# Packed weights shared by batches 0 and 1 from block 1 on, a one-instruction gate in units 10–28, 115–128 and 180–255, and moved plan times

## The chip, the cores and the metric

The kernel runs on one core of one Trainium2 chip. The metric is device time in microseconds (us), the median of three runs. Five engines work side by side, each through its own queue in order: PE (TensorE, matrix products), DVE (VectorE), ACT (ScalarE), POOL (GpSimd) and SP (SyncE, which here only issues DMAs). All share the core's 16 DMA engines.

## The reference, cut to what matters

Two attentions in a row, then two feed-forward layers, all in f32:

```python
p_packed = sm_attn(p, k, v)            # 32 packed queries a head, over 576 keys
out = sm_attn(q, p_packed, p_packed)   # 576 queries over those 32
x = out as (8*576, 8*64)               # 4608 tokens, 512 features
h = x @ w_in                           # 512 -> 2048
g = h * (1 / (1 + exp(-1.702 * h)))    # the gate
x = g @ w_out                          # 2048 -> 512
h = max(x @ w1, x @ w2, x @ w3)        # 512 -> 768
out = h @ w_out2                       # 768 -> 512
```

Batch 8, heads 8, head width 64.

## The kernel before

**Numbers.** Every f32 operand of a large product is split into a high and a low part, and `mm3` (lines 97 to 102) makes three matmuls of it: high by low, low by high, high by high.

**Packed weights.** The second attention's output is never multiplied with `w_in` itself. `p_packed` of a batch is multiplied with `w_in` once, which gives the packed weights `pw[b, n]` of batch b and block n (512 of the 2048 hidden features; n is 0 to 3). The first feed-forward product of the batch is then attention weights (`at`) by `pw`. Two code paths make `pw`. For batches 2 to 7, `pw_unit` (line 402) takes two batches at once: their packed rows stand interleaved in a tile `sp`, so three matmuls of 512 columns serve a pair, and the result is evacuated in two halves of 64 partitions, each by an ACT copy (high part) and a DVE subtraction (low part). For batches 0 and 1, `pw1_unit` (line 418) works on one batch: its tiles `pt` hold zeros beside the packed rows, so six matmuls are made where the pair path makes three, and the evacuation is over 128 partitions at once. Both paths take their accumulator from `ps_a`, two PSUM tiles that the attention's scores, transposes and sums also use.

**Units.** The first feed-forward layer runs in 256 units n of (batch, half of the tokens, 128 hidden features). `h_unit` makes six matmuls of 288 columns (`h<-at,pw`) into one of two PSUM tiles, ACT takes a tanh of it and DVE joins both to `(1 + tanh) * h` (lines 460, 461), which is twice the gate. `g_unit` splits that: ACT writes the high part, DVE (POOL for the first two units) the low part. `out_unit` makes twelve matmuls (`acc<-g,wo`), two units later on PE, and halves the sum when it evacuates it. Batches 0 and 1 hold units 0 to 63, in the pattern batch 0 block 0, batch 1 block 0, batch 0 block 1, batch 1 block 1, then blocks 2 and 3 of batch 0 (from unit 32) and of batch 1 (from unit 48).

**The start.** Weights are converted on the chip from the 32-bit form they arrive in (`convert`, `convert_low`: chains of DVE instructions over 128x1024 with two ACT passes). In the first 60 us DVE converts the first blocks of `w_in` and `w_out` while it also runs the softmaxes of the attention groups (batch, half of the heads): (0,0), (0,1), (1,0), (1,1). The exponentials are ACT's `Exp` (lines 259 and 340).

**What sets the order.** Every piece of work is put into `plan` with a time, and the plan is recorded in order of time (`main`, lines 804 to 925): tables such as `D_`, `K_`, `L_`, `W_`, `Q_` and `R_` shift single steps. A scheduler then settles each engine's own order. Nothing waits for a clock: an instruction runs when those ahead of it on its engine are issued and its inputs are there. The second feed-forward layer (`Set`, `out2`) takes the last 550 us; no line of it is touched.

Of the kernel before, what the change touches and what calls it, by code (L numbers as in the profile page):

```python
# [19 lines left out]
P = 128  # L20
# [10 lines left out]
SCALE = 1.0 / D ** 0.5  # L31
D_ = [-2, -8, 2.9, -2.51, 2.83, -0.47, -3.58, -0.6, 0.92, -0.32, -6.66, 0.91, 2.97, 2.32, -5.59, -0.32]
W_ = [60, 15.02, 42.09, 0]
K_ = [2, 11, -8, 6, 1, -7, 10, 6, -11, -14, -9, -5, -2, -13, -1, 4]
L_ = [8.18, 16.49, 4, 22.39]
Z_ = [1, 1, 1, 0, 0, 0, 0, 0, 0, 0, 0, 0, 0, 0, 0, 0]
PL_ = [10, 12]
Q_ = [12, 9, 9, 8]
R_ = [32, 23, 17, 5]
TP_ = [6.0, 8.5, 5.0]  # L40


@with_exitstack
def tile_packed_attention_moe(
# [159 lines left out]
    class Group:  # L204
# [91 lines left out]
        def pt(self):  # L296
# [86 lines left out]
    def pw_unit(pr, c, n):  # L383
# [65 lines left out]
    part = {}  # L449

    def h_unit(n):
        b, hf, fc = units[n]
        o = ps_h.tile([P, TB], F32, tag="ph", name=f"h_{n}")[:, :HALF]
        hs = slice(hf * HALF, hf * HALF + HALF)
        fs = slice(fc % 4 * P, fc % 4 * P + P)
        for g in range(2):
            w = pw[b, fc // 4][:, g]
            mm3(o, (w[:, 0, fs], w[:, 1, fs]), [t[:, hs] for t in at[b, g]], g == 0, g == 1)
        t = gp.tile([P, HALF], F32, tag="t", name=f"t_{n}")
        nc.scalar.activation(t, o, AF.Tanh, scale=0.5 * 1.702)  # L460
        nc.vector.scalar_tensor_tensor(out=t, in0=t, scalar=1.0, in1=o, op0=ALU.add, op1=ALU.mult)  # L461
        gt[n] = t

    def g_unit(n):
        g = gp.tile([P, 2, HALF], F32R, tag="g", name=f"g_{n}")
        latest["act"] = nc.scalar.copy(g[:, 0], gt[n])  # L466
        eng = nc.gpsimd if n < 2 else nc.vector
        latest["dve"] = eng.tensor_tensor(out=g[:, 1], in0=gt[n], in1=f(g[:, 0]), op=ALU.subtract)  # L468
        gt[n] = g

    def out_unit(n):
# [3 lines left out]
        for dc in range(KD):  # L475
# [328 lines left out]
    def main():  # L804
        HU = 2.2
        T0 = 39

        add(-2.0, keep_busy, 28)
        attention(0.0, 0, 0, 1.07)
        attention(8, 0, 1, 1.07)  # L810
        attention(20, 1, 0, 0.97, 0)
        attention(34, 1, 1, 0.97, 0)

# [3 lines left out]
        for n in range(N1 + 2):  # L817
# [30 lines left out]
        for n in range(NQ):  # L848
# [3 lines left out]
            for g in range(2):  # L852
# [68 lines left out]
        for n in range(9 * NBLK):  # L921
# [85 lines left out]
```

## Time and profile before

| | |
|---|---|
| median of 3 runs | 1334.27 us (1333.46 to 1334.63) |
| the profiled execution, its own time | 1333.64 us |
| its span (first to last instruction) | 1331.5 us |
| PE busy | 1308.8 us, 98% |
| DVE busy | 919.9 us, 69% |
| ACT busy | 533.3 us, 40% |
| POOL busy | 107.4 us, 8% |
| instructions | 22347 |

Busy is the time in which an engine has an instruction at work, and a busy PE is not PE at its peak, since matmuls overlap. How long a matmul holds PE is read from the distance between two starts. Idle time of an engine counts only where another waits for it.

### The profile page before, as it was taken

How to read it: one execution, taken by the hardware profiler on the slowest of the kernel's cores; microseconds unless marked ns; L12 is line 12 of the kernel's file. 1: busy time of each engine (PE TensorE's matmuls, PEld its weight loads, DVE VectorE, ACT ScalarE, POOL GpSimd, SP SyncE). 2: the span in 40 equal slices, each digit the busy share in tenths (PEclk: the TensorE clock that was granted, in tenths of full speed). 3: DMA queues.
4: the chain of work that ended last, by engine and by line, in shares of the span. 5: the costliest groups of instructions: out<-in, count | busy, mean ns of one | idle time of the engine just before them, and what ended most of it. 6: DMA issues, size and time to landing. Idle time of an engine off the chain costs nothing.

```text
span 1331.5 us, 22347 instructions
## 1 busy us (share of the span) xinstructions
PE 1308.8 (98%) x8614; PEld 1229.7 (92%) x8614; DVE 919.9 (69%) x1896; ACT 533.3 (40%) x1140; POOL 107.4 (8%) x218
## 2 busy tenths in 40 slices
PE   6899999999999999999999999999999999999998
PEld 5699898989999989999999999999899899999997
DVE  6899976874756565669999889736556467366461
ACT  3466544554445444446656442311311313123111
POOL 1200001100000000000000001001011011010000
PEclk9899999999999999999999999999999999999999
DMA  9697734643323331236655649847657476575451
GB/s 338 211 403 300 251 107 139 193 123 120 106 80 100 103 102 54 82 112 195 207 200 191 206 160 360 294 169 252 223 188 264 151 261 239 172 254 197 174 174 48
DMA packets 88875, 249.70 MB, mean 188 GB/s; under 512 B 10177, under 2 KB 39361, under 8 KB 81857
## 3 DMA queue, kind: packets, MB, share of 16 engines
q0 software_dynamic: 24640, 132.66, 29.2%
q1 hardware_dynamic: 64128, 115.62, 25.4%
q8 instruction: 68, 1.11, 0.3%
q14 instruction: 39, 0.31, 0.1%
HBM read 204.47 MB, written 43.78 MB: 186 GB/s over the span
## 4 chain that ended last, share of the span: by engine, by line
PE 92%; DVE 4%; DMA 2%; issue 1%; ACT 1%; SPq 0%; POOL 0%; ACTq 0%; DVEq 0%; POOLq 0%
PE acc L100 10%; PE p L101 10%; PE p L100 10%; PE p L102 10%; PE acc L102 10%; PE acc L101 9%; PE h L100 5%; PE h L102 5%; PE h L101 5%; PE accb L101 4%; PE accb L102 4%; PE accb L100 4%; PE pw L100 1%; PE pw L101 1%; PE pw L102 1%; PE pv L287 1%
## 5 line engine op out<-in xcount | busy, mean ns | idle before, releaser
L100 PE MATMUL acc<-g,wo 128*128 128x288 f32 x1024 | 303.6, 299 | 0.0
L102 PE MATMUL acc<-g,wo 128*128 128x288 f32 x1024 | 300.6, 294 | 0.0
L101 PE MATMUL acc<-g,wo 128*128 128x288 f32 x1024 | 299.6, 293 | 0.4 <-POOL g L468 0.3
L100 PEld LDWEIGHTS acc<-g,wo 128*128 128x128 f32 x1024 | 191.4, 188 | 10.5 <-issue 5.3
L101 PEld LDWEIGHTS acc<-g,wo 128*128 128x128 f32 x1024 | 192.2, 188 | 4.3 <-issue 1.0
L102 PEld LDWEIGHTS acc<-g,wo 128*128 128x128 f32 x1024 | 192.0, 188 | 1.6 <-issue 1.5
L460 ACT ACTIVATE t<-h 128x288 f32<-128x288 f32 x256 | 104.8, 410 | 181.7 <-PE h L102 179.8
L461 DVE SCALAR_TENSOR_TENSOR t<-t,h 128x288 f32<-128x288 f32 x256 | 114.7, 450 | 84.7 <-ACT t L460 83.3
L100 PE MATMUL h<-at,pw 128*128 128x288 f32 x512 | 155.2, 304 | 1.3 <-DVE t L461 1.1
L101 PE MATMUL h<-at,pw 128*128 128x288 f32 x512 | 151.7, 296 | 0.3 <-POOL at L125 0.3
L102 PE MATMUL h<-at,pw 128*128 128x288 f32 x512 | 151.3, 296 | 0.0
L466 ACT CAST g<-t 128x288 fp32r<-128x288 f32 x256 | 110.6, 433 | 93.6 <-DVE t L461 92.4
L468 DVE TENSOR_TENSOR g<-t,g 128x288 fp32r<-128x288 f32 x254 | 114.9, 453 | 34.7 <-ACT g L466 33.8
L681 DVE TENSOR_TENSOR u<-s,p 128x384 f32<-128x384 f32 x54 | 29.9, 553 | 119.1 <-PE p L102 119.1
L101 PE MATMUL p<-x_T,ws 128*128 128x384 f32 x324 | 108.2, 334 | 0.0
L100 PE MATMUL p<-x_T,ws 128*128 128x384 f32 x324 | 108.2, 334 | 0.0
L102 PE MATMUL p<-x_T,ws 128*128 128x384 f32 x324 | 108.1, 334 | 0.0
L100 PEld LDWEIGHTS h<-at,pw 128*128 128x128 f32 x512 | 96.3, 188 | 9.7 <-issue 5.6
L101 PEld LDWEIGHTS h<-at,pw 128*128 128x128 f32 x512 | 96.4, 188 | 1.7 <-POOL at L125 1.3
L102 PEld LDWEIGHTS h<-at,pw 128*128 128x128 f32 x512 | 96.4, 188 | 0.1
L711 ACT COPY s<-p 128x384 f32<-128x384 f32 x54 | 25.9, 479 | 161.8 <-PE p L102 161.7
L129 DVE TENSOR_TENSOR pw<-pw,pw 64x512 fp32r<-64x512 f32 (+1 forms) x110 | 74.9, 686 | 18.2 <-ACT pw L128 17.2
(175 smaller groups left out, 2637.1 us busy)
## 6 DMA issues: line engine op xcount, KB each, us to landing
ws<-wss POOLq DMA_DIRECT2D x54, 1024.0 KB, 7.6
wa<-wsa POOLq DMA_DIRECT2D x54, 768.0 KB, 4.6
wi<-wsc POOLq DMA_DIRECT2D x48, 512.0 KB, 3.9
k<-in_k SPq DMA_DIRECT2D x16, 576.0 KB, 4.2
q<-in_q SPq DMA_DIRECT2D x16, 576.0 KB, 3.9
x2d<-x SPq DMA_DIRECT2D x16, 576.0 KB, 4.0
wss<-ws SPq DMA_DIRECT2D x36, 256.0 KB, 4.0
xr<-x2d SPq DMA_DIRECT2D x24, 384.0 KB, 4.1
```

What stands on the lines that cost most here:

```text
L100: nc.tensor.matmul(o, al, bh, start=start, stop=False, skip_group_check=more)
L101: nc.tensor.matmul(o, ah, bl, start=False, stop=False, skip_group_check=more)
L102: nc.tensor.matmul(o, ah, bh, start=False, stop=stop, skip_group_check=more)
L129: nc.vector.tensor_tensor(out=lo, in0=o, in1=f(hi), op=ALU.subtract)
L287: self.mm = nc.tensor.matmul(o[x * D:x * D + D, :P], self.et[:, c * P + x * D:c * P + x * D + D], self.v[:, c, y * P:y * P + P], start=c = ...
L460: nc.scalar.activation(t, o, AF.Tanh, scale=0.5 * 1.702)
L461: nc.vector.scalar_tensor_tensor(out=t, in0=t, scalar=1.0, in1=o, op0=ALU.add, op1=ALU.mult)
L466: latest["act"] = nc.scalar.copy(g[:, 0], gt[n])
L468: latest["dve"] = eng.tensor_tensor(out=g[:, 1], in0=gt[n], in1=f(g[:, 0]), op=ALU.subtract)
L681: latest["dve"] = nc.vector.tensor_tensor(out=o, in0=a, in1=b, op=op)
L711: latest["act"] = nc.scalar.copy(self.s1, self.b1)
```

## The change

Five things are done:

1. For blocks 1 to 3 of batches 0 and 1 `pw_unit` replaces `pw1_unit`: the group step `pt` copies each batch's packed rows into a shared `sp` tile (four POOL copies of 128x64 a group, sixteen in all), and four units of three matmuls serve a block of both batches. Block 0 stays with `pw1_unit`. Block 2 and 3 of batch 1 are now made together with those of batch 0, ahead of unit 32.
2. In units 10 to 28, 115 to 128 and 180 to 255 (`direct`) ACT makes the gate with one function, `Gelu_apprx_sigmoid`, and DVE's joining instruction is gone. ACT switches its function table at the ends of these stretches.
3. In the other units the factor 0.5 moves from the evacuation of the sum into `g_unit`; instruction counts stay.
4. The low part of units 0 and 1 moves from POOL to DVE.
5. The plan's tables get other numbers, `D_` one row a group; the first block of `w_in` is loaded ahead of the first keys.

```diff
-L_ = [8.18, 16.49, 4, 22.39]
+L_ = [11.39, 16.49, 4, 22.39]
...
+G_ = [10, 29, 115, 129, 180]
...
+            if self.b < 2:
+                for x in range(2):
+                    for c in range(2):
+                        d = (c ^ self.b) * P + c * D
+                        nc.gpsimd.tensor_copy(sps[key][x][:, d:d + D], f(to[x][:, c * 192:c * 192 + D]))
...
+    def direct(n):
+        return G_[0] <= n < G_[1] or G_[2] <= n < G_[3] or n >= G_[4]
...
-        nc.scalar.activation(t, o, AF.Tanh, scale=0.5 * 1.702)
-        nc.vector.scalar_tensor_tensor(out=t, in0=t, scalar=1.0, in1=o, op0=ALU.add, op1=ALU.mult)
+        if direct(n):
+            latest["act"] = nc.scalar.activation(t, o, AF.Gelu_apprx_sigmoid)
+        else:
+            nc.scalar.activation(t, o, AF.Tanh, scale=0.5 * 1.702)
+            nc.vector.scalar_tensor_tensor(out=t, in0=t, scalar=1.0, in1=o, op0=ALU.add, op1=ALU.mult)
...
-        eng = nc.gpsimd if n < 2 else nc.vector
-        latest["dve"] = eng.tensor_tensor(out=g[:, 1], in0=gt[n], in1=f(g[:, 0]), op=ALU.subtract)
+        if direct(n):
+            latest["act"] = nc.scalar.copy(g[:, 0], gt[n])
+            latest["dve"] = nc.vector.tensor_tensor(out=g[:, 1], in0=gt[n], in1=f(g[:, 0]), op=ALU.subtract)
+        else:
+            latest["act"] = nc.scalar.mul(g[:, 0], gt[n], 0.5)
...
-                for b in range(2):
-                    add(max(t + .1, tn[start[b, n]] - PL_[b], tpt[b, g]), pw1_unit, b, g, n)
+                for x in range(2):
+                    if n < PAIR0:
+                        add(max(t + .1, tn[start[x, n]] - PL_[x], tpt[x, g]), pw1_unit, x, g, n)
+                    else:
+                        add(max(t + .1, tn[start[0, n]] - 10 + 2 * x, tpt[1, g]), pw_unit, 0, 2 * g + x, n)
```

**DVE at the start.** In the names the two numbers behind a word are batch and group; `praw` is what a DMA brings of the packed queries, `pbd` the copy that needs it, `a` and `at` the second softmax, `wo2` a block of `w_out` under conversion. Before, in DVE's queue:

```order
L356 STREAM_TRANSPOSE at_0_0_467<-a_0_0_369 128x576
L263 TENSOR_SCALAR st1_1_0_427<-st1_1_0_427 128x1
L266 RECIPROCAL st1_1_0_427<-st1_1_0_427 128x1
L330 STREAM_TRANSPOSE a_0_1_476<-s2_0_1_0_473 128x288
L330 STREAM_TRANSPOSE a_0_1_476<-s2_0_1_1_478 128x288
L220 COPY pbd_2_0_1622<-praw_2_0_1593 64x2x32 x2
L336 TENSOR_REDUCE st2_0_1_482<-a_0_1_476 128x18
L337 TENSOR_TENSOR a_0_1_476<-a_0_1_476,st2_0_1_482 128x576
```

And now:

```order
L350 STREAM_TRANSPOSE a_0_1_476<-s2_0_1_1_478 128x288
L356 TENSOR_REDUCE st2_0_1_482<-a_0_1_476 128x18
L185 TENSOR_SCALAR tmp_wo2_529<-raw_wo2_249 128x1024
L357 TENSOR_TENSOR a_0_1_476<-a_0_1_476,st2_0_1_482 128x576
L188 TENSOR_SCALAR tmp_wo2_529<-raw_wo2_249 128x1024
L191 SCALAR_TENSOR_TENSOR tmp_wo2_529<-raw_wo2_249,tmp_wo2_529 128x1024
L189 SCALAR_TENSOR_TENSOR tmp_wo2_529<-raw_wo2_249,tmp_wo2_529 128x1024
L195 TENSOR_SCALAR raw_wo2_249<-tmp_wo2_529 128x1024
L366 TENSOR_REDUCE st2_0_1_482<-a_0_1_476 128x18
L196 SCALAR_TENSOR_TENSOR wo2_530<-tmp_wo2_529,raw_wo2_249 128x2x512
L367 TENSOR_SCALAR st2_0_1_482<-st2_0_1_482 128x18
L231 COPY pbd_2_0_1585<-praw_2_0_1514 64x2x32 x2
```

The copy for group (2,0) has moved behind the conversion of `wo2` and the larger part of group (0,1)'s softmax.

**DVE around unit 32.** Here `pw_b_n` is a block's packed weights, `t` and `g` belong to the unit whose number follows. Before:

```order
L461 SCALAR_TENSOR_TENSOR t_32_1805<-t_32_1805,h_32_1798 128x288
L156 TENSOR_SCALAR low_wo12_1674<-low_wo12_1674 128x1024
L129 TENSOR_TENSOR pw_0_3_1808<-pw_0_0_3_1809,pw_0_3_1808 128x512
L129 TENSOR_TENSOR pw_0_3_1808<-pw_0_1_3_1818,pw_0_3_1808 128x512
L468 TENSOR_TENSOR g_32_1839<-t_32_1805,g_32_1839 128x288
L158 SCALAR_TENSOR_TENSOR raw_wo12_1522<-raw_wo12_1522 128x1024
```

And now:

```order
L173 TENSOR_SCALAR raw_wo12_1511<-raw_wo12_1511 128x1024
L140 TENSOR_TENSOR pw_0_3_1834<-pw_0_0_3_1836,pw_0_3_1834 64x512
L140 TENSOR_TENSOR pw_0_3_1834<-pw_0_2_3_1844,pw_0_3_1834 64x512
L497 SCALAR_TENSOR_TENSOR g_32_1876<-t_32_1831,g_32_1876 128x288
L140 TENSOR_TENSOR pw_1_3_1835<-pw_0_0_3_1836,pw_1_3_1835 64x512
L140 TENSOR_TENSOR pw_1_3_1835<-pw_0_2_3_1844,pw_1_3_1835 64x512
```

Two evacuations of 128 partitions have become eight of 64 (four more stand a few rows on), and block 3 of batch 1, which stood near unit 48 before, is among them.

**ACT at unit 10.** Before:

```order
L466 CAST g_9_976<-t_9_956 128x288
L460 ACTIVATE t_10_989<-h_10_982 128x288
L466 CAST g_10_1008<-t_10_989 128x288
L460 ACTIVATE t_11_1021<-h_11_1014 128x288
L154 ACTIVATE raw_wo6_1011<-raw_wo6_1011,rebias_100 128x1024
```

And now:

```order
L496 ACTIVATE g_9_995<-t_9_975 128x288
L139 CAST pw_0_1_1068<-pw_0_2_1_1078 64x512
L484 ACT_TABLE_LOAD
L484 ACTIVATE t_10_1008<-h_10_1001 128x288
L139 CAST pw_1_1_1069<-pw_0_0_1_1070 64x512
L493 CAST g_10_1026<-t_10_1008 128x288
```

A table load stands ahead of unit 10's gate; ACT's queue holds six loads in all, one before.

## Rows read from the trace of the kernel before

**Rows 1.** The page: busy time of each engine; DVE in 40 slices, tenths.
```profile
PE 1308.8 (98%) x8614; PEld 1229.7 (92%) x8614; DVE 919.9 (69%) x1896; ACT 533.3 (40%) x1140; POOL 107.4 (8%) x218
...
DVE  6899976874756565669999889736556467366461
```

**Rows 2.** Busy time by stretch: length, engines (count), granted clock, DMA share, GB/s.
```profile
10.00:20.00 10.00, 7.04 (x74) 5.89 (x72) 7.26 (x15) 4.03 (x9) 0.21 (x1) 0.86 1.03 392
...
0.00:61.20 61.20, 45.31 (x369) 33.75 (x369) 45.99 (x92) 26.69 (x57) 10.77 (x32) 0.92 0.80 286
61.20:172.30 111.10, 110.52 (x788) 101.30 (x787) 103.00 (x196) 67.38 (x133) 9.46 (x13) 1.00 0.79 298
172.30:222.80 50.50, 49.91 (x368) 44.15 (x366) 37.47 (x89) 23.28 (x58) 2.66 (x7) 1.00 0.40 123
...
600.00:780.00 180.00, 178.82 (x1324) 176.27 (x1324) 171.85 (x409) 106.13 (x234) 3.72 (x7) 1.00 0.56 184
```

**Rows 3.** The chain that ended last, first 62 us: start, length, what.
```profile
4.09 7.47 DMA praw<-in_p
...
35.98 5.51 DMA praw<-in_p
...
52.70 1.42 POOL at L125
...
57.53 0.40 PE acc L101
```

**Rows 4.** DVE in order of time: start, length, [idle before <- what ended it].
```profile
7.11 0.46 DVE L250 TENSOR_REDUCE st<-s 128x1 f32<-128x288 f32 x1 [3.96 <-PE s L242]
...
11.66 0.19 DVE L220 COPY pbd<-praw 64x64 f32<-64x64 f32 x1 [3.12 <-DMA praw<-in_p]
...
18.44 1.22 DVE L185 SCALAR_TENSOR_TENSOR wi<-tmp_wi,raw_wi 128x1024 fp32r<-128x1024 f32 x1
...
41.58 0.39 DVE L220 COPY pbd<-praw 64x64 f32<-64x64 f32 x2 [2.72 <-DMA praw<-in_p]
...
171.84 0.45 DVE L468 TENSOR_TENSOR g<-t,g 128x288 fp32r<-128x288 f32 x1
```

**Rows 5.** ACT in order of time, around 47 us.
```profile
47.09 0.59 ACT L274 COPY et<-t 128x512 f32<-128x512 f32 x1
...
48.19 1.05 ACT L183 CAST wo<-tmp_wo 128x1024 fp32r<-128x1024 f32 x1
```

**Rows 6.** PE in order of time, at six places.
```profile
44.80 1.11 PE L273 MATMUL t<-ident,e 128*128 128x128 f32 x4 [2.99 <-ACT pw L410]
...
64.59 0.39 PE L102 MATMUL pw<-wi,pt 128*128 128x512 f32 x1
64.82 0.39 PE L100 MATMUL pw<-wi,pt 128*128 128x512 f32 x1
...
172.69 0.29 PE L100 MATMUL acc<-g,wo 128*128 128x288 f32 x1
...
223.07 0.47 PE L100 MATMUL pw<-wi,sp 128*128 128x512 f32 x1 [0.86 <-DMA wi<-wsc]
...
626.63 0.40 PE L100 MATMUL h<-at,pw 128*128 128x288 f32 x1 [0.88 <-DVE t L461]
```

**Rows 7.** Groups by line and shape: busy us, mean ns | idle before, released by.
```profile
L461 DVE SCALAR_TENSOR_TENSOR t<-t,h 128x288 f32<-128x288 f32 x256 | 114.7, 450 | 84.7 <-ACT t L460 83.3
L129 DVE TENSOR_TENSOR pw<-pw,pw 64x512 fp32r<-64x512 f32 x96 | 65.7, 687 | 17.3 <-ACT pw L128 16.5
L100 PE MATMUL pw<-wi,sp 128*128 128x512 f32 x48 | 19.3, 403 | 1.0 <-DMA wi<-wsc 0.9
L129 DVE TENSOR_TENSOR pw<-pw,pw 128x512 fp32r<-128x512 f32 x14 | 9.2, 683 | 0.9 <-ACT pw L128 0.7
L112 ACT ACT_TABLE_LOAD x1 | 1.3, 1283 | 0.7 <-PEq L996 0.7
```

**Rows 8.** Waits over the whole run: engine and line, for whom, us, times, longest.
```profile
ACT t L460 <- PE h L102: 179.8, 182, 3.2
```

More of the change, by code (lines that the diff above doesn't have):

```diff
@@ L31 @@
 SCALE = 1.0 / D ** 0.5
[L32 to L35 removed]
+W_ = [51.57, 15.02, 42.09, 0]
+K_ = [0.99, 11, -8, 6, 1, -7, 10, 6, -11, -14.16, -9, -5, -1.38, -11.62, -1, -0.78]
+L_ = [11.39, 16.49, 4, 22.39]
 Z_ = [1, 1, 1, 0, 0, 0, 0, 0, 0, 0, 0, 0, 0, 0, 0, 0]
 PL_ = [10, 12]
[L38 removed]
+Q_ = [11, 8, 9, 11]
 R_ = [32, 23, 17, 5]
[L40 removed]
+TP_ = [6.78, 8.5, 5.08]
+D_ = [[-2, -8, 2.9, -2.75, 2.83, -0.47, -6.25, -0.6, 0.92, -0.32, -6.66, 0.91, 6.48, 3.62, -5.59, -0.32], [-2, -8, 2.9, -2.51, 2.83, -0.47, -3.58, -0.6, 1.5, -0.32, -6.66, 0.61, 2.97, 1.15, -5.59, -0.32], [7.94, -7.26, 2.9, -2.51, 2.83, -0.47, -3.58, -0.6, 0.92, -0.32, -6.66, 0.91, 2.97, 2.32, -2.6, -0.32], [-2, -8, 2.9, -2.51, 2.83, -0.47, -3.58, -2.71, 5.52, -0.32, -9.11, 0.91, 2.97, 2.32, -5.59, -0.32]]
+A_ = [0.0, 8, 20, 34]
+AS_ = [1.05, 1.06, 0.97, 0.97]
+T_ = [39, 1.23, 1.16, 11]
+B2_ = [66.3, 18, 1.2, 5.85]
+B4_ = [20, 2, 1.2, 39.32]
+PC_ = [-8, 4.26, 5, 6.37, 9, 14, 10, 10.5]
+G_ = [10, 29, 115, 129, 180]
+X_ = [252, 2.6]
+PAIR0 = 1
+D1 = 0
 @with_exitstack
@@ L304, in pt @@
                 to = ptt[self.b, self.g] = [t[:, HALF * x:HALF * x + 2 * P] for x in range(2)]
+                key = 0, self.g
+                if key not in sps:
+                    t = u_tile(f"sp_{self.g}", F32R)
+                    sps[key] = [t[:, HALF * x:HALF * x + 2 * P] for x in range(2)]
             else:
@@ L465, in g_unit @@
         g = gp.tile([P, 2, HALF], F32R, tag="g", name=f"g_{n}")
-        latest["act"] = nc.scalar.copy(g[:, 0], gt[n])
-        eng = nc.gpsimd if n < 2 else nc.vector
-        latest["dve"] = eng.tensor_tensor(out=g[:, 1], in0=gt[n], in1=f(g[:, 0]), op=ALU.subtract)
+        if direct(n):
[3 more added lines that the diff above has]
+            latest["act"] = nc.scalar.mul(g[:, 0], gt[n], 0.5)
+            latest["dve"] = nc.vector.scalar_tensor_tensor(
+                out=g[:, 1], in0=gt[n], scalar=0.5, in1=f(g[:, 0]), op0=ALU.mult, op1=ALU.subtract
+            )
         gt[n] = g
@@ L487, in out_unit @@
             if old is not None:
-                nc.vector.scalar_tensor_tensor(
-                    out=x2[:, dc], in0=o, scalar=0.5, in1=x2[:, dc], op0=ALU.mult, op1=ALU.add
-                )
+                nc.vector.tensor_tensor(out=x2[:, dc], in0=o, in1=x2[:, dc], op=ALU.add)
             elif dc % 2 == 0:
-                nc.scalar.mul(x2[:, dc], o, 0.5)
+                nc.scalar.copy(x2[:, dc], o)
             else:
-                nc.vector.tensor_scalar(out=x2[:, dc], in0=o, scalar1=0.5, scalar2=None, op0=ALU.mult)
+                nc.vector.tensor_copy(x2[:, dc], o)
         if n in last:
@@ L797, in attention @@
             after = {9: 7, 13: 12, 12: 11, 11: 10, 10: 8, 8: 6, 6: 5, 5: 3, 3: 1, 4: 2, 1: 0}.get(k)
-            tk = t + dt * stretch + (D_[k] if b == 0 else 0) + (dq if k in (7, 9, 11, 12, 13) else 0)
+            tk = t + dt * stretch + (D_[2 * b + g][k] if b == 0 or b == 1 and D1 else 0) + (dq if k in (7, 9, 11, 12, 13) else 0)
             ts.append(tk if after is None else max(tk, ts[after] + .05))
@@ L805, in main @@
         HU = 2.2
-        T0 = 39
+        T0 = T_[0]
         add(-2.0, keep_busy, 28)
[L809 to L812, printed above, removed]
+        attention(A_[0], 0, 0, AS_[0])
+        attention(A_[1], 0, 1, AS_[1])
+        attention(A_[2], 1, 0, AS_[2], 0)
+        attention(A_[3], 1, 1, AS_[3], 0)
         N1 = 2 * B * NFC
@@ L824, in main @@
                 add(t + HU / 2 + .01, g_unit, n)
-            t += (1.23 * HU) if n < 11 else HU * 1.16
+            t += (T_[1] * HU) if n < T_[3] else HU * T_[2]
         TB0 = t
@@ L901, in main @@
             pc = Piece(idx // 2, idx % 2)
-            t = TP + idx * TP_[1] if idx < 14 else TB0 - 10 + (idx - 14) * 10.5
+            t = TP + idx * TP_[1] if idx < 14 else TB0 - PC_[6] + (idx - 14) * PC_[7]
             for dt, fn in (
-                (-8 if idx > 1 else -TP_[0] + .2, pc.load), (0, pc.conv), (4, pc.sums), (5, pc.save_a),
-                (6.5, pc.split_hi), (9, pc.split_lo),
+                (PC_[0] if idx > 1 else -TP_[0] + .2, pc.load), (0, pc.conv), (PC_[1], pc.sums), (PC_[2], pc.save_a),
+                (PC_[3], pc.split_hi), (PC_[4], pc.split_lo),
             ):
@@ L926, in main @@
             if n == 0:
-                add(tn[252], load_set, n)
+                add(tn[X_[0]], load_set, n)
             elif n < 3:
```

6 lines of the change are left out of this document (3 added, 3 removed).

## The prediction

> **What bounds the kernel now.** First the profile's page: PE is busy 98% of the span, DVE 69%, ACT 40% [rows 1]. DVE's slices are not even: 9 tenths in slices 3 to 5 and 19 to 22, mostly 4 to 7 between. So PE is the bound on the whole, with DVE beside it at the start and near 600 to 780 us. Next the busy times by stretch [rows 2]. Until 61.2 us PE has work for 45.3 us and DVE for 46.0: nobody is full, the start is a chain of waits. From 61.2 to 172.3 us PE has 110.5 of 111.1 and DVE 103.0: PE sets the pace, but DVE has only 8.1 us to spare. From 172.3 to 222.8 DVE has 13 us to spare. From 600 to 780 PE lacks 1.2 us and DVE 8.2. Elsewhere PE is full, and a microsecond of PE work is a microsecond of time. The chain of the first 62 us [rows 3] is DVE's queue broken by two landings of `praw` (7.47 and 5.51 us), and ends in POOL's split of `at` for group (0,1) and the first `acc` at 57.53.
>
> **PE work.** Blocks 1 to 3 of batches 0 and 1 cost 3 x 24 = 72 matmuls of 512 columns before and 3 x 12 = 36 now. Two such matmuls start 64.82 - 64.59 = 0.23 us apart [rows 6], so the 36 are worth 36 x 0.23 = 8.3 us of PE. By unit 37 only 12 of them are gained (2.8 us): before, blocks 2 and 3 of batch 1 came near units 48 and 52, now they come ahead of 32 and 36. The other 24 (5.5 us) are gained by unit 52. As both stretches are PE's, all 8.3 us count, unless something else is late. The Trainium skill, page "TensorE: Matmul & The Clock Gate", section "Back-to-back issue gap", gives a sustained roofline of about 131 ns a matmul at N=512 in a stream of weight loads and matmuls; by it the term would be an estimated 36 x 0.131 = 4.7 us and the time 3.6 us more than mine; this trace has 0.23 us between starts and decides against it.
>
> **The start.** Two DVE waits stand in the chain [rows 4]. The first is 3.12 us before the copy at 11.66. Now the raw `w_in` block (1 MB) is loaded ahead of the keys, so the first keys land later by about 1.05 MB / 392 GB/s = 2.7 us [rows 2], and the first reduction moves from 7.11 to about 9.7 us; behind it the conversion of `w_in` fills what was the wait. From 9.7 I add DVE's instructions up to the end of that conversion and the two reductions of group (0,1): 0.39 + 0.61 + 0.39 + 0.61 + 0.5 (small ones) + 1.14 + 1.14 + 0.61 + 1.14 + 0.2 + 0.73 = 7.5, so 17.2 us; before, the same point is 18.44 + 1.22 = 19.66 [rows 4]. Lead 2.5 us. The second wait, 2.72 us before 41.58, hangs on a DMA issued at 35.98 (5.51 us) [rows 3]; the copy now stands behind some 8 us of other DVE work, which hides the landing. Lead at most 5.2 us. Next late is ACT: the cast of `wo` (1.05 us, at 48.19) stood behind the copies of `et` (47.09) [rows 5] and now stands ahead of them, waiting for DVE's conversion, so group (1,0)'s sums and what follows on DVE come about 1.1 us later than DVE alone would let them. And DVE takes two `g` subtractions from POOL, 0.8 us. I take a lead of 3.0 us at the first `acc`; bounds: a loss of 2.7 us, if the late keys push the whole chain, and a gain of 5.2.
>
> **DVE between units 2 and 37.** Ahead of g_37 DVE's queue now holds 24 half evacuations where 8 full ones stood; a half takes as long as a full one, 687 against 683 ns [rows 7]. That is 16 x 0.687 = 11.0 us more, a conversion step (1.2 us) stands earlier, and 19 joining instructions of the gate are gone, 19 x 0.45 = 8.6 us: 3.7 us more in all. Before, g_37 starts on DVE at 171.84 and its `acc` on PE at 172.69 [rows 4, 6]. PE wants that `acc` 3.0 + 2.8 us earlier, at 166.9. DVE would have g_37 done at 172.3 - 3.0 + 3.7 = 173.0 if none of its 8.1 us of idle time closes, at 164.9 if all does. So PE loses between 0 and 6.1 us. I take half of the idle time as closing, since most of it is waits for ACT's `t`, which waits for PE: 169.0, a loss of 2.1 us. From 172 to 223 DVE has its 13 us to spare and fewer evacuations to do, so nothing more is lost there.
>
> **Other stalls.** PE's 0.86 us before 223.07 is a wait for a loaded `wi` [rows 6]; the matmuls of that unit now stand one `out_unit` and one `h_unit` later in PE's queue, 18 matmuls of 288 columns, and I count the wait as gone: -0.9 (bounds 0 and -0.9). PE's 0.88 us before 626.63 waits for DVE's joining instruction to free the `h` tile; from unit 180 on ACT frees it and 76 x 0.45 us leave a DVE that was busy 171.9 of 180 us: -0.9 (same bounds).
>
> **At nothing.** The table loads: five more of 1.28 us [rows 7]. ACT waits 179.8 us for `h` in 182 waits, about 1 us each [rows 8], and a load needs no input, so it runs in such a wait; `acc` is two units behind. Without that cover it is 5 x 1.28 = 6.4 us. The page "ScalarE: Activation LUTs", section "What ACT_TABLE_LOAD costs", of the Trainium skill puts a switch at about 2.66 us with its drain and advises to do all calls of one set before switching; the one load in this trace shows 1.28 us, with ACT idle around it. The sixteen POOL copies lie in POOL's idle time (8% busy); the same factor on other instructions costs nothing. The second layer is untouched.
>
> **The sum**, on the profiled execution's 1333.64 us: -8.3 - 3.0 + 2.1 - 0.9 - 0.9 = -11.0, so 1322.6. The median of the runs shown is 0.6 above that execution; I forecast 1323.3 us.
>
> **Rivals.**
> - *PE stays full.* DVE's idle time closes entirely and the start gives its 5.2 us: -8.3 - 5.2 - 0.9 - 0.9 = -15.3, 1319.0 us. For it: most DVE waits in the stretch are for PE's results. Against: ACT's cast in the start.
> - *DVE takes the stretch.* None of its idle time closes: loss 6.1 us, the wait at 223 stays: -8.3 - 3.0 + 6.1 - 0.9 = -6.1, 1328.2 us. For it: 103.0 of 111.1 us is little room, and the halves come earlier than before.
> - *Every table switch reaches PE* at the skill's full price: an ACT held at each of the five ends, 5 x 2.66 = 13.3 us in an estimate, 1336.6 us and no measurable change; by the row's 1.28 us it would be 1329.7. Against: ACT is idle 60% of the time.
> - *The `ps_a` tiles jam: slower.* The twelve pair units want one of two `ps_a` tiles each 0.7 us, and a tile now comes free only after two ACT and two DVE halves. PE has stood 2.99 us before 44.80 for just that [rows 6]. If six of the twelve units wait so long, 17.9 us are lost in place of the 2.1: 1323.3 - 2.1 + 17.9 = 1339.1. From the fifth such wait it is slower than before, from the sixth measurably. Against: 48 pair units of batches 2 to 7 waited only 1.0 us together before their first matmul, 0.9 of it for a DMA [rows 7].
>
> That the pairing does not do what it says is out: PE's queue holds 36 matmuls fewer.
>
> **How the numbers follow.** Forecast 0.52 (1320.5 to 1326), PE stays full 0.20, DVE takes the stretch 0.18, table switches 0.04, jam 0.04, others 0.02. About 0.2% (2.7 us) is what a measurement here can tell from no change: faster means below 1331.6, slower above 1336.9. The first three are faster save for their tails: 0.91; same 0.05 (table switches and a start at its worst bound); slower 0.04. The range reaches from just under PE stays full to past DVE takes the stretch, 1318.5 to 1329.5.
>
> **What would show it.** PE with 36 matmuls fewer (8578). The first `acc` near 54.5 us, and no DVE wait for `praw` near 40. g_37 near 169 us, DVE nearly full until there. PE's waits before 223 and 627 gone. Six table loads, none with PE idle behind it. I am wrong if the first `acc` is not earlier than 57.5, if PE shows waits for `pw` evacuations between units 9 and 36, or if units 180 to 255 run slower than before.

## The result and the profile after

The changed kernel takes 1344.70 us (median of 4 runs, 1343.88 to 1346.83), the kernel before beside it 1334.28 us: 1.0081 times as long, 95% interval 1.0064 to 1.0099. Forecast were 1323.3 us, 1318.5 to 1329.5. The profiled execution took 1343.88 us. In it the changed kernel leads by 5.1 us at unit 180, where about 10 were forecast, and the loss arose later, in two places: 11.7 us between units 180 and 231, and 5.1 us at the start of the second layer.

The page after: span, busy time of each engine, DVE in 40 slices, the chain by engine.

```profile
span 1342.1 us, 22135 instructions
...
PE 1307.6 (97%) x8578; PEld 1226.7 (91%) x8578; DVE 892.4 (66%) x1801; ACT 549.2 (41%) x1157; POOL 112.4 (8%) x232
...
DVE  7899977855654565678878568736646467366461
...
PE 81%; DMA 7%; DVE 7%; ACT 1%; issue 1%; SPq 1%; POOL 0%; DVEq 0%; ACTq 0%; POOLq 0%
```

The 36 matmuls are gone (8578 for 8614, [rows 1]) and DVE has 27.5 us less to do. Yet DVE's slices 19 to 22, all 9 before, are now 8, 8, 7, 8, and a seventh of the chain is now DMA or DVE. An engine that was relieved stands idle there, and waits for transfers.

Busy time by stretch after (columns as in [rows 2]):

```profile
0.00:61.20 61.20, 44.70 (x390) 32.96 (x391) 48.08 (x96) 27.88 (x58) 15.93 (x44) 0.92 0.80 286
61.20:172.30 111.10, 107.68 (x753) 99.10 (x753) 105.52 (x189) 78.21 (x148) 9.35 (x16) 0.98 0.80 298
172.30:222.80 50.50, 50.50 (x401) 46.13 (x402) 37.46 (x94) 23.72 (x60) 3.49 (x9) 1.00 0.44 140
600.00:780.00 180.00, 172.36 (x1242) 168.39 (x1242) 142.59 (x323) 100.58 (x222) 2.66 (x5) 0.98 0.54 178
785.00:830.00 45.00, 41.75 (x246) 41.38 (x245) 35.24 (x78) 13.68 (x27) 5.81 (x11) 0.96 0.84 283
```

From 600 to 780 us DVE falls from 171.85 to 142.59 us, and PE, which should have gained, falls from 178.82 to 172.36 us. PE's waits between units 180 and 231 add up to 7.5 us, for 1.1 before. The mean granted clock is 0.98 in that row, for 1.00 before: two stretches at the lower clock, from 629 and from 728 us, make an estimated 3 to 4 of the 11.7 us (0.02 of 180 us). From 785 to 830 PE lacks 3.25 us.

Where the kernels stand in time, from the starts of the first `acc` matmul of a unit (the matmuls `acc<-g,wo` come twelve to a unit) and the end of PE's last matmul:

| us | unit 0 | 37 | 60 | 180 | 231 | 255 | PE's end |
|---|---|---|---|---|---|---|---|
| before | 56.9 | 172.7 | 252.8 | 600.0 | 729.3 | 785.4 | 1327.5 |
| after | 55.8 | 174.3 | 244.9 | 594.9 | 735.8 | 791.2 | 1338.5 |
| late gate off (e2) | 55.2 | 173.8 | 244.4 | 594.4 | 725.6 | 781.2 | 1333.4 |
| late times back (e3) | 57.1 | 175.6 | 246.2 | 594.8 | 738.3 | 794.1 | 1336.2 |
| late gate off, late times back (e4) | 55.8 | 174.3 | 244.9 | 593.5 | 723.0 | 779.1 | 1321.3 |
| steps held (e5) | 55.4 | 174.0 | 244.6 | 595.5 | 726.0 | 782.0 | 1324.2 |
| late gate alone (e13) | 59.6 | 175.4 | 255.2 | 602.4 | 747.6 | 804.0 | 1346.2 |

The changed kernel leads by 7.9 us at unit 60 and by 5.1 at unit 180, and is 6.5 behind at unit 231.

**What is waited for.** Waits from 590 to 735 us (engine and line, for whom, us, times, longest), of after, DVE and then ACT:

```profile
DVE c L548 <- DMA wraw<-in_w: 15.7, 10, 3.5
DVE c_o L548 <- DMA wraw_o<-in_w_out: 3.3, 3, 2.1
...
ACT c L549 <- DVE c L548: 15.6, 10, 4.0
```

and of before, the one such wait:

```profile
DVE c L519 <- DMA wraw<-in_w: 1.3, 1, 1.3
```

`wraw` is the raw form of a piece of `w1` to `w3`, which is converted in the shadow of units 180 to 240. There are two such buffers. DVE's last step on a piece (`wa<-c,wraw`, L557) frees its buffer, SP issues the load of the piece after next into it, and DVE's first step on that piece (`c<-wraw`, L548) reads it. One such turn in after, in order of time, with what queued behind it on DVE, ACT and PE:

```profile
688.68 0.68 DVE L557 SCALAR_TENSOR_TENSOR wa<-c,wraw 128x512 fp32r<-128x512 f32 x1
689.29 0.68 DVE L605 TENSOR_TENSOR ws<-c,ws 128x512 fp32r<-128x512 f32 x1
689.89 0.84 DVE L494 TENSOR_TENSOR g<-t,g 128x288 fp32r<-128x288 f32 x2
690.65 0.69 DVE L586 TENSOR_TENSOR c<-c,wa 128x512 f32<-128x512 f32 x1
...
695.91 0.43 DVE L548 TENSOR_SCALAR c<-wraw 128x512 int32<-128x512 int32 x1 [3.52 <-DMA wraw<-in_w]
...
696.59 0.45 DVE L494 TENSOR_TENSOR g<-t,g 128x288 fp32r<-128x288 f32 x1
...
696.38 0.72 ACT L549 ACTIVATE c<-c,rebias 128x512 int32<-128x512 int32 x1 [2.81 <-DVE c L548]
697.00 0.39 ACT L484 ACTIVATE t<-h 128x288 f32<-128x288 f32 x1
...
697.10 0.40 PE L112 MATMUL acc<-g,wo 128*128 128x288 f32 x1 [0.89 <-DVE g L494]
```

The same turn, of the same piece, in before (L528 frees, L519 reads; the rows between are cut to the joining instructions):

```profile
688.08 0.68 DVE L528 SCALAR_TENSOR_TENSOR wa<-c,wraw 128x512 fp32r<-128x512 f32 x1
...
690.26 0.44 DVE L461 SCALAR_TENSOR_TENSOR t<-t,h 128x288 f32<-128x288 f32 x1
...
692.14 0.44 DVE L461 SCALAR_TENSOR_TENSOR t<-t,h 128x288 f32<-128x288 f32 x1
...
694.53 0.45 DVE L461 SCALAR_TENSOR_TENSOR t<-t,h 128x288 f32<-128x288 f32 x1
...
695.23 0.42 DVE L519 TENSOR_SCALAR c<-wraw 128x512 int32<-128x512 int32 x1
```

In after the buffer is free at 689.4, its load lands at 695.8, and DVE starts instructions of 2.7 us in between and then stands 3.52 us. A gate subtraction is queued behind it on DVE, ACT's step on the piece waits with it and holds the next gate, and PE runs dry. In before the two instructions stand 6.5 us apart with DVE full, and the load, 5.9 us from free to landed, is over 0.55 us before it is asked for; in the other turns of before it is over 0.35 to 9.7 us ahead. Over the twelve turns of the first 14 pieces, from the end of the freeing instruction to the last of the piece's three landings, and the summed lengths of the DVE instructions that start between the freeing and the reading one (they overlap, so DVE's busy time is about a tenth less):

| us | free to landed | DVE's work between, mean (range) | turns with less work than load |
|---|---|---|---|
| before | 6.2 (4.4 to 8.6) | 10.6 (5.2 to 16.7) | 0 |
| after | 6.2 (4.4 to 8.4) | 5.4 (2.7 to 8.1) | 9 |
| e2, late gate off | 6.6 (4.4 to 8.7) | 9.3 (5.0 to 17.2) | 1 |
| e5, steps held | 6.7 (4.6 to 7.9) | 11.9 (10.0 to 15.8) | 0 |
| e13, late gate alone | 6.3 (4.5 to 8.2) | 4.8 (4.1 to 5.9) | 11 |

**The start of the second layer.** After, DVE and PE in order of time:

```profile
807.00 0.55 DVE L710 TENSOR_TENSOR m<-u,p 128x384 f32<-128x384 f32 x1 [5.58 <-DMA wss<-ws]
...
808.74 0.45 PE L111 MATMUL p<-x_T,wa 128*128 128x384 f32 x1 [3.25 <-DVE u L710]
```

The chain of after there, and in the start (start, length, what):

```profile
50.66 1.43 POOL at L136
...
56.59 0.41 PE acc L112
...
794.61 12.30 DMA wss<-ws
```

`m` has nothing to do with the store `wss<-ws`. But the second layer's tiles lie on memory that the first layer's pool `up` gave back, and by the addresses that the program gives its tiles the third `m` tile that DVE writes lies on the low part `ws1` of piece 7_0, which is just being stored. The store takes 12.30 us among the weight sets that are loaded then. In the kernel before no `m` tile of the first set lies on a tile of that piece's stores.

### The profile page after: what moved, and what is told of

It is laid out like the page before. It is cut to its first block, busy times and chain, and to the rows that moved or that the text cites. A ratio compares the mean times of both kernels' runs of the same rounds, so it can differ in the third digit from the quotient of the medians.

```text
span 1342.1 us, 22135 instructions
## 1 busy us (share of the span) xinstructions
PE 1307.6 (97%) x8578; PEld 1226.7 (91%) x8578; DVE 892.4 (66%) x1801; ACT 549.2 (41%) x1157; POOL 112.4 (8%) x232
## 4 chain that ended last, share of the span: by engine, by line
PE 81%; DMA 7%; DVE 7%; ACT 1%; issue 1%; SPq 1%; POOL 0%; DVEq 0%; ACTq 0%; POOLq 0%
PE p L113 10%; PE p L111 10%; PE p L112 10%; PE acc L111 8%; PE acc L113 8%; PE acc L112 8%; PE h L111 4%; PE h L112 4%; PE h L113 4%; PE accb L113 4%; PE accb L112 4%; PE accb L111 4%; DMA wraw<-in_w 3%; PE pv L298 1%; PE s L253 1%
## 5 line engine op out<-in xcount | busy, mean ns | idle before, releaser
L487 DVE SCALAR_TENSOR_TENSOR t<-t,h 128x288 f32<-128x288 f32 x147 | 66.1, 451 | 66.1 <-ACT t L486 64.9
L486 ACT ACTIVATE t<-h 128x288 f32<-128x288 f32 x147 | 60.4, 411 | 118.9 <-PE h L113 117.8
L140 DVE TENSOR_TENSOR pw<-pw,pw 64x512 fp32r<-64x512 f32 (+1 forms) x122 | 82.9, 686 | 18.0 <-ACT pw L139 16.1
L139 ACT CAST pw<-pw 64x512 fp32r<-64x512 f32 (+1 forms) x122 | 70.4, 581 | 39.7 <-DVE pw L140 27.1
L496 ACT ACTIVATE g<-t 128x288 fp32r<-128x288 f32 x147 | 65.2, 445 | 52.1 <-DVE t L487 51.8
```

What stands on the lines that cost most here:

```text
L139: nc.scalar.copy(hi, o)
L140: nc.vector.tensor_tensor(out=lo, in0=o, in1=f(hi), op=ALU.subtract)
L496: latest["act"] = nc.scalar.mul(g[:, 0], gt[n], 0.5)
```

## Experiments

### The late loss: gate or plan times

Two single edits and both together. e2, the late gate off, and e3, the late plan times back:

```diff
-G_ = [10, 29, 115, 129, 180]
+G_ = [10, 29, 115, 129, 256]
```

```diff
-TP_ = [6.78, 8.5, 5.08]
+TP_ = [6.0, 8.5, 5.0]
-B4_ = [20, 2, 1.2, 39.32]
+B4_ = [20, 2, 1.2, 38]
-PC_ = [-8, 4.26, 5, 6.37, 9, 14, 10, 10.5]
+PC_ = [-8, 4, 5, 6.5, 9, 14, 10, 10.5]
```

> The changed kernel with the one-instruction gate off from unit 180 on: units 180 to 255 have tanh and DVE's joining instruction again; all else as changed. Theory A (the late gate is the cause: with 76 x 0.45 us less work DVE reaches the first step of each weight piece before its raw data has landed, stands there 15.7 us in 10 waits, and ACT and the units queue behind): the 12.6 us that PE loses between units 190 and 231 come back, the first layer ends near 785.4 + 5.8 = 791.2 - 12.6 - less than 1, that is 6 us earlier than before the change; the whole 1332.1 us, or up to 5 less or more as the memory of the first m tiles falls. Here the first m tile (not the third) lies on the late ws1 tile, so a stall of 5 to 9 us at the start of the second layer is to be seen. Rival B (the moved plan times of the late pieces are the cause): DVE waits for raw data as long as now, 1343 to 1346 us.

> The changed kernel with the plan times of the late pieces and of the last attentions as they were (TP_ 6.0, 8.5, 5.0; steps at -8, 4, 5, 6.5, 9; 38 for 39.32); the late gate stays on. Here no m tile of the first set lies on a late ws tile. Theory A (the late gate is the cause): only the stall at the start of the second layer goes, 1344.7 - 5.1 = 1339.6 us, DVE still waits over 10 us for raw data between 590 and 735 us. Rival B (the moved times are the cause): both go, 1344.7 - 12.6 - 5.1 = 1327.0 us.

> Both edits: late gate off and late plan times as before the change. What is left of the change is the pairing, the gate in units 10 to 28 and 115 to 128 and the moved times of the start. Both theories: the loss from 600 us on is gone and the lead of the first 600 us (5 to 7 us) stays: 1334.3 - 6 = 1328.3 us, 1326.5 to 1330. If it stays over 1334, neither the late gate nor the late times make the loss.

Measured: e2 1339.67 us (ratio to before 1.0044, 1.0027 to 1.0060), e3 1341.88 us (1.0064, 1.0049 to 1.0079), e4 1327.26 us (0.9953, 0.9938 to 0.9968). DVE's waits from 590 to 735 us in e2, and in e3:

```profile
DVE c L548 <- DMA wraw<-in_w: 1.6, 2, 1.4
```

```profile
DVE c L548 <- DMA wraw<-in_w: 19.8, 12, 3.8
```

In e2 unit 255 comes at 781.2 us, 10.0 earlier than after, and the second layer then takes 10.0 us more than in e4 (552.2 for 542.2 from unit 255 to PE's end), since here the first `m` tile lies on the store and PE stands 7.11 us (timeline of e2):

```profile
797.05 0.55 DVE L710 TENSOR_TENSOR m<-u,p 128x384 f32<-128x384 f32 x1 [10.41 <-DMA wss<-ws]
...
797.66 0.69 PE L111 MATMUL p<-x_B,ws 128*128 128x384 f32 x1 [7.11 <-DVE m L710]
```

e3 keeps DVE's waits, and PE is full from 785 us to 830: no `m` tile waits for a store there. So the gate makes the late loss and the times do not. The times cost a little elsewhere: units 60 to 180 take 350.0 us in after and in e2, and 348.6 in e3 and e4. With both back, e4 beats both kernels; its page has PE at 1300.1 us, 8.7 less than before, and from 600 us on it looks like before:

```profile
600.00:780.00 180.00, 178.92 (x1325) 176.20 (x1324) 171.33 (x404) 105.10 (x229) 3.71 (x7) 1.00 0.54 178
785.00:830.00 45.00, 45.00 (x260) 44.82 (x260) 38.90 (x85) 12.02 (x24) 6.36 (x12) 1.00 1.01 366
```

### The late gate alone, in the kernel before

```diff
+        if n >= 180:
+            latest["act"] = nc.scalar.activation(t, o, AF.Gelu_apprx_sigmoid)
+        else:
...
+            latest["act"] = nc.scalar.mul(g[:, 0], gt[n], 2.0)
```

> The kernel before with one part of the change alone: the one-instruction gate from unit 180 on (the factor 2 that keeps the sum as it was goes into g_unit; counts of the other instructions stay). No m tile of the first set lies on a late store. Theory A (the joining instructions were what hid the reload of the raw buffers): DVE waits over 10 us for raw data between 590 and 735 us where the kernel before waits 1.3, the first layer ends 10 to 15 us later than 785.4, the whole 1344 to 1349 us. Forecast of the prediction, which counted on a gain there: 1332.7 us. Rival (the loss came only together with the moved times or the pairing): within 2 us of 1333.6.

Measured 1348.37 us (1.0115, 1.0098 to 1.0132). DVE's waits from 590 to 735 us:

```profile
DVE c L528 <- DMA wraw<-in_w: 19.7, 12, 3.0
```

One edit that takes 76 joining instructions away, and adds one table load, costs 15 us, by itself and without any moved time.

### The late gate with the cover put back

```diff
+            if self.k < 7:
+                with tc.issue_after(latest["dve"].ins):
+                    self.v, self.s = conv_late(self.n, self.raw, *self.hl, TB)
+                return
             self.v, self.s = conv_late(self.n, self.raw, *self.hl, TB)
```

> The changed kernel, late gate and late times left on; only the first DVE step of each of the first 14 late weight pieces is tied behind the unit at its own plan time, so that DVE runs more units between the step that frees a raw buffer and the step that reads it again: 5 or 6 units for 1 to 3 (before the change: 4 to 6). Theory A (a raw buffer takes 4.4 to 8.7 us from being freed to being loaded again, and without the joining instructions DVE has only 2.7 to 8.1 us of work between, 5.2 to 16.7 before): DVE's 15.7 us of waits for raw data fall under 4, the 12.6 us that PE lost between units 190 and 231 come back. No m tile of the first set lies on a late ws tile, so the 5.1 us at the start of the second layer go too: 1344.7 - 12.6 - 5.1 = 1327 us, 1325 to 1330. Rival C (it is ACT's longer queue, the new function and the switch of its table, that makes the units late): waits for raw data go but PE still loses over 8 us between units 190 and 231, 1337 to 1340 us.

Measured 1331.33 us (0.9979, 0.9969 to 0.9989). The late gate is on, DVE does 149.55 us of work from 600 to 780, and PE has its time back:

```profile
600.00:780.00 180.00, 177.63 (x1317) 175.06 (x1316) 149.55 (x336) 107.77 (x231) 2.68 (x5) 1.00 0.56 184
```

DVE waits 1.2 us for raw data in all. Of 11.7 us lost between units 180 and 231 it gets 10.5 back, and the stall at the second layer's start is gone too. This is the experiment that shows the mechanism: no work was added, the read was only put behind more of the units. It stays 4 us above e4 and above its own expectation. By PE's end in the traces it is 2.9 us; 2.0 of them are there by unit 180, ahead of the edit, in a kernel that still has the moved late times. The rest was not followed further.

> The kernel of the run with gate off and times back (1327.3 us), with the one-instruction gate on again from unit 236 on, where the first 14 weight pieces are converted and only two pieces are left before the second layer. Theory A (the late gate costs only where raw buffers are turned over): DVE waits for raw data no more than 2 us between 590 and 735, the whole within 1.5 us of 1327.3. Rival C (the one-instruction gate itself makes units late, through ACT): 20 of 76 units of the loss, some 3 us or more: 1330 to 1332 us.

Edit: `G_[4]` at 236 in e4. Measured 1328.54 us (0.9961, 0.9947 to 0.9976), DVE waits 1.2 us for raw data. The one-instruction gate costs nothing that can be measured where no buffer is turned over, and gains nothing either, as PE is full.

### The stall at the second layer

> The changed kernel with one edit: the two output tiles of one late piece of w1 to w3 (ws0 and ws1 of piece 7_0) change places in memory. No engine's order of instructions changes. In the changed kernel the third m tile of the second layer lies on the memory of ws1_7_0, whose store is issued at 794.6 us and lands at 806.9; DVE stands 5.58 us before 807.00 and PE 3.25 us before 808.74. With the edit that m lies on ws0_7_0, whose store lands at 801.2. Theory (a wait for reused memory): DVE's wait falls to nearly nothing, PE's 3.25 us and the lower clock behind it (together 5.1 us of PE time) go, 1344.7 - 5.1 = 1339.6 us. Rival (the second layer starts late because its weight sets and the stores share the DMA engines): the wait only takes another name, 1344.7 us, within 1.5.

Edit: `self.shl.reverse()` for piece 7_0. Measured 1341.57 us (1.0062, 1.0047 to 1.0077), and DVE's wait is 5.69 us as before the edit. The experiment failed: by the addresses that the program gives, the exchange changed two names and the low part stayed where it was. What it is worth is a second measurement of the changed kernel, 3 us from the first, so a difference of that size between two medians shows little by itself.

> The changed kernel with the late tile ws1 of piece 7_0 taken from another pool, so that no m tile of the first set lies on memory with a store under way (the exchange of the two names before had left the low part where it was, as the same wait showed). The conversion of piece 7_1 moves behind the end of the first layer by it. Theory (a wait for reused memory): DVE's 5.6 us and PE's 3.25 us at the start of the second layer go, the first layer stays as it is (last acc near 791): 1344.7 - 5.1 = 1339.6 us, perhaps 1 more for the moved piece. Rival (DMA contention by itself): PE still stands over 2 us between 785 and 830, 1343 to 1346 us.

Edit: `ws1` of piece 7_0 from the pool `late["r"]`. Measured 1345.27 us (1.0087, 1.0072 to 1.0103). The third `m` no longer waits for a store, but piece 7_1, moved behind the units by the edit, brought three other waits for stores that take 12 to 15 us there, and PE stands 4.6 us in two of them. It moved too much to tell the theories apart.

```diff
+            if self.n == "7_0":
+                self.spare = u_tile("spare")
+                nc.gpsimd.memset(self.spare[:, :1], 0.0)
```

> The changed kernel with a spare tile of the same pool allocated and touched by POOL (two one-column memsets) between the two late tiles ws0 and ws1 of piece 7_0, so that ws1 falls on other memory and no m tile of the first set lies on a store under way. Apart from the two memsets each engine's order is the changed kernel's, and no transfer moves. Theory (a wait for reused memory): the third m tile is written when its product is there, PE's 3.25 us before 808.74 and the low clock behind it go, the first layer ends as now near 791: 1344.7 - 5.1 = 1339.6 us. Rival (the set loads and stores that share the DMA engines hold the second layer up in any case): another wait of 2 us or more between 785 and 830, 1343 to 1346 us.

Measured 1338.66 us (1.0038, 1.0024 to 1.0052). The third `m` now waits for its product alone, and PE is full (timeline and windows of e9):

```profile
801.10 0.55 DVE L715 TENSOR_TENSOR m<-u,p 128x384 f32<-128x384 f32 x1 [0.35 <-PE p L113]
```

```profile
785.00:830.00 45.00, 45.00 (x275) 45.00 (x274) 40.28 (x90) 13.81 (x27) 7.55 (x16) 1.00 0.92 321
```

The transfers and each engine's order are those of the changed kernel, but for two one-column memsets on POOL. By the traces the nine sets of the first block end 5.1 us earlier against the first layer's end, as early as in before; by the medians the whole is 6.0 us shorter than after and 2.9 shorter than e1. Only where one tile lies was changed: it was the memory.

### The first 240 us: pairing and early gate

> The kernel of the run with gate off and times back (1327.3 us), with the pairing undone: blocks 1 to 3 of batches 0 and 1 by the single path again, 36 more matmuls of 512 columns and 16 evacuation pairs fewer (the sixteen POOL copies stay). Theory (PE's 8.3 us count, part of it is given back before unit 37 because DVE has 24 halves for 8 full evacuations): unit 37 comes earlier than 174.3 us by 1 to 3, unit 60 later than 244.9 us by 4 to 7, the whole 1331 to 1334 us. Rival (the halves eat all of it): within 1 us of 1327.3.

> The kernel of the run with gate off and times back (1327.3 us), with the one-instruction gate off in units 10 to 28 and 115 to 128 too: 19 joining instructions of 0.45 us come back before unit 37, and no function table is switched. Theory (DVE sets the pace of units 28 to 37): unit 37 comes later than 174.3 us by 3 to 8, the whole 1330 to 1335 us. Rival (DVE has the room; what units 28 to 37 wait for is ACT or the evacuations): within 1.5 us of 1327.3. If the table switches cost, it becomes faster: 1321 to 1326.

Edits in e4: `PAIR0 = 4`, and all of `G_` at 256. Measured: pairing off 1336.44 us (1.0019, 1.0009 to 1.0029), early gate off 1334.32 us (1.0008, 0.9996 to 1.0021). From 61.2 to 172.3 us, e7 and then e8:

```profile
61.20:172.30 111.10, 107.82 (x776) 99.81 (x775) 96.85 (x183) 69.29 (x133) 10.13 (x17) 1.00 0.79 298
```

```profile
61.20:172.30 111.10, 103.54 (x711) 92.68 (x710) 107.52 (x197) 72.48 (x138) 9.31 (x16) 1.00 0.79 298
```

Neither is worth anything without the other. The pairing alone takes 36 matmuls from PE but leaves DVE with 107.52 of 111.10 us, and DVE takes the gain back (1334.3). The gate alone frees a DVE that was not the limit (1336.4; unit 60 at 252.8 us, as before). Together they bring 7 to 9 us. Both kernels keep the moved times of the start, which no run took back alone, so what these are worth is not shown. The expectation for e7 had unit 37 earlier without the pairing; it came at 181.2 us, 6.9 later than in e4, so with the early gate the halves cost less than the matmuls that they replace even there.

> The kernel of the run with gate off and times back (1327.3 us), with the four pair units of a block planned 4 apart, from 14 ahead of the block's first unit, for 2 apart from 10 ahead. In the changed kernel PE stands 1.90 us at 144.06 for a g that ACT makes behind four half evacuations, and runs at half clock for some 3.5 us behind it. Theory (the jam of half evacuations ahead of unit 32 is what unit 37 lost, about 4 us): the wait at 144 falls under 0.8 us, unit 37 comes 2 to 4 us earlier than 174.3, the whole 1323.5 to 1325.5 us. Rival (DVE as a whole is short before unit 37, the place does not matter): the wait moves, within 1.5 us of 1327.3.

> The kernel of the run with gate off and times back (1327.3 us), with the pair units planned from 7 ahead of the block's first unit instead of 10. Theory D (the place counts: the half evacuations press on ACT and DVE while units 28 to 31 want their gates; earlier lost 5.5 us): later wins 1 to 4 us, 1323.5 to 1326.5, PE's wait at 144 gets shorter. Rival E (DVE's whole work before unit 37 counts, and any move only shifts the wait): the wait comes nearer to unit 32, 1327 to 1332 us.

> The kernel of the run with gate off and times back (1327.3 us), with the first stretch of the one-instruction gate reaching to unit 36 in place of 28: eight joining instructions of 0.45 us less on DVE, two table switches more (ACT, 1.28 us each), right in the stretch where DVE is short. Rival E (DVE's whole work counts): unit 37 comes 2 to 4 us earlier than 174.3, the whole 1323.5 to 1325.5 us. Theory D (place, or ACT): a switch stands ahead of g or of a half evacuation on ACT's queue and eats it, 1327 to 1330 us.

Edits in e4: the pair units at `- 14 + 4 * x`, at `- 7 + 2 * x`, and `G_[1]` at 37. Measured 1332.85 us (0.9996, 0.9987 to 1.0005), 1328.81 us (0.9963, 0.9949 to 0.9977), 1327.33 us (0.9951, 0.9937 to 0.9966). The expectation for e11 fell: earlier places cost 5.6 us, and PE waits at nine places from 62 to 175 us, 6.9 us in all, where e4 has five and 3.4 us. Later ones cost about 1.5 us, no more than two medians can differ by. Eight joining instructions less changed nothing that can be measured; the wait at 144 us went, one of 1.11 us at 169 came. So of the three places tried none is better than the one in the change, and what DVE still lacks there is small.

e15 also loads ACT's function table seven times where e4 does five times and e8 once. One of its groups:

```profile
L360 ACT ACT_TABLE_LOAD x1 | 1.3, 1283 | 0.0
```

No switch shows in the time. The Trainium skill, page "ScalarE: Activation LUTs", section "What ACT_TABLE_LOAD costs", counts 2.66 us for each; the loads here are the 1283 ns that it gives for the load itself. After the load at 167.50 us in e15 ACT's next instruction starts at 168.80, so 1.30 us is all that this switch took, and e15 beside e4 (1327.33 and 1327.26 us) shows no two switches of 2.66 us on the path, unless the eight joining instructions gave back as much.

> The kernel of the run with gate off and times back (1327.3 us), with the low part of units 0 and 1 on POOL again, as before the change (POOL halves t first, 0.6 us more). In the changed kernel POOL's split of at for group (0,1) ends 2.0 us earlier than before, the first acc only 1.0 us earlier, because DVE's low part of unit 0 stands behind a reduction of group (1,0). Theory (that DVE place costs the start 1.0 us): first acc near 55 us, the whole 1326.5 us. Rival (POOL's extra halving and its slower subtraction eat it): first acc not earlier than 55.5 us, within 1 us of 1327.3 or slower.

Edit in e4: the low part of units 0 and 1 on POOL. Measured 1328.16 us (0.9954, 0.9941 to 0.9968), first `acc` at 56.1 us for 55.8. The theory found no support; but kernels with one and the same start differ by more than 1 us there (next section), so a cost of that size could hide.

## Why the prediction was wrong

**The step that failed** is the last of "Other stalls": "from unit 180 on ACT frees it and 76 x 0.45 us leave a DVE that was busy 171.9 of 180 us: -0.9 (same bounds)". It measured +11.7 us (units 180 to 231, 129.3 us before and 141.0 after). Its first half came true, PE's wait at 627 for the joining instruction is gone (PE waits there for `x`, which ACT and DVE evacuate late, 1.42 and 0.66 us). But the bounds, 0 and -0.9, took work that is removed from a full engine to be harmless at worst. DVE's queue also held reads of two buffers that a load of 4.4 to 8.7 us had to refill, and the joining instructions were what lay between. The rows to see it were there: DVE waits just once for `wraw` before, 1.3 us, and 96% busy with hardly a wait for a transfer says that something covers each load. The prediction asked for the cover of what it added, not for what the removed work covered. None of the four rivals was this one, though slower units from 180 to 255 stood among the signs of being wrong.

**"The second layer is untouched"** is the other step: true of the code, not of the memory. The change allots other tiles in `up` and moves late pieces, and a tile of the second layer came to lie on a store under way: +5.1 us in the changed kernel (PE's 3.25 us and the low clock behind it); e9 is 6.0 us faster than after by the medians, and 2.9 faster than e1.

**PE work, -8.3**: held. PE is 8.7 us less busy in e4 than before, and between e7 and e4, where the early gate makes room for it, the pairing is worth 7.6 us by PE's end in the two traces (1328.9 and 1321.3 us) and 9.2 by the medians. The Trainium skill's figure (page "TensorE: Matmul & The Clock Gate", section "Back-to-back issue gap") gave an estimate of 4.7; both measurements decide for the distance in the rows.

**The start, -3.0**: the first half as worked out. The conversion and the two reductions end at 17.2 us, as forecast, and the two waits for `praw` that it counted are gone. POOL's split for (0,1) starts at 50.66 for 52.70 [rows 3], a lead of 2.0, the `acc` matmul of the chain at 56.59 for 57.53, a lead of 0.9. Where the last 1.1 us went was not found (e10), and kernels with this same start have their first `acc` anywhere from 55.2 to 58.1 us, so the term is smaller than its own scatter.

**DVE before unit 37, +2.1**: right in kind, low in size. Summed over PE's starts, what lies beyond the distance of a full PE (0.13 us for 288 columns, 0.23 for 512) grew from 6.5 to 10.5 us between 60 and 180 us: +4.0, within the bounds 0 to 6.1. Most of it is one wait, of a `g` that ACT makes behind half evacuations and a cast, and the clock after it. So the sign "g_37 near 169 us" failed: DVE starts g_37 at 173.6 us, later than before the change (171.8), and PE's `acc` of unit 37 comes at 174.3 for 172.7, with 20 attention matmuls (`pv`, some 1 us) moved ahead of it.

**The wait at 223, -0.9**: gone. **Table loads, 0**: held. **`ps_a` jam, switches, DVE takes the stretch**: none of them decided; the third is what e8 shows when the early gate is missing.

Up to unit 60 the sum was -10.1 and the lead measured 7.9. Of that, 2.8 us are given back by unit 180; half of it is the moved late times (e3 and e4 give back 1.4 less), and where the other 1.4 us go was not followed. Without the two late steps the forecast would have been 1324 against e4's 1327.3 us.

## What to carry over

Before taking work from an in-order engine, look for what that work covers: for each buffer that is turned over in the stretch, compare the engine's work between the instruction that frees it and the one that reads it again with the time from free to landed. An engine at 96% with hardly a wait for a transfer may be hiding loads behind its work; take work away, and hold the reads back by as many units as the work was worth. And a tile added early can move what lies where much later, so look at the waits of the first writes after each pool is released.

## What the hardware showed besides

A short wait of PE can cost about 2 us more than itself. Windows of after around the wait that ends at 144.06, and around the one that ends at 808.74 (granted clock third from the end):

```profile
143.00:144.00 1.00, 0.00 (x0) 0.00 (x0) 0.70 (x2) 0.98 (x2) 0.00 (x0) 1.00 1.01 414
144.00:145.00 1.00, 0.94 (x6) 0.94 (x7) 0.97 (x3) 0.01 (x1) 0.00 (x0) 0.85 1.02 409
145.00:148.00 3.00, 3.00 (x14) 2.75 (x12) 2.27 (x5) 1.77 (x4) 0.00 (x0) 0.50 0.71 281
```

```profile
806.00:808.00 2.00, 0.00 (x0) 0.00 (x0) 0.99 (x2) 0.00 (x0) 0.00 (x0) 1.00 1.07 386
...
810.00:814.00 4.00, 4.00 (x16) 4.00 (x15) 4.00 (x10) 1.62 (x3) 1.06 (x2) 0.57 0.69 246
```

The clock is at its upper level (2.4 GHz) in the wait itself and falls to the lower one (1.2 GHz, 0.50) about a microsecond after PE is at work again, for some 3 us. So a wait of 1.90 us cost about 4 us, and one of 3.25 us cost 5.1. But not every such wait has this fall behind it. In e12, where PE waits 1.90 us for the same `g`, up to 146.07 us, the clock stays at 1.00:

```profile
146.00:147.00 1.00, 0.93 (x7) 0.94 (x8) 0.97 (x3) 0.01 (x1) 0.00 (x0) 1.00 1.01 414
147.00:150.00 3.00, 2.93 (x33) 2.42 (x31) 2.73 (x6) 1.78 (x4) 0.00 (x0) 1.00 0.60 240
```

In e3 a wait of 3.10 us before 598.23 has no fall behind it either, nor has the one of 0.88 us before 626.63 in [rows 6] (the clock is 1.00 from 600 to 780 us, [rows 2]). What decides it was not found. e4, with the fall, takes 189.1 us from unit 0 to unit 60, and e12, with the same order of work up to there and no fall, 188.0.

The store `wss<-ws` of 256 KB, which lands in 3.0 us in the median of its 36, took 12.30 us while the loads of two weight sets and two other stores were under way.
